# Routing logits of a fused attention and mixture-of-experts kernel: the gate's weight held in four column groups, and eight subtractions on GpSimd

## The chip, the cores and the metric

The kernel runs on one core of a Trainium2 chip. The metric is the device time of one execution in microseconds (us). The kernel before has a median of 2101.33 us over three runs (2100.89 to 2102.82).

## The reference, cut to what matters

Attention with 4 sink keys and a window of 128 (4 batches, 8 heads, 768 positions, 64 wide) gives x of 3072 tokens by 512. From x come the routing logits, which eight rounds of row and column scaling turn into the weights P of 8 experts; the output is the sum of P times each expert's result. The change touches the line that forms the logits, and the preparation of one expert's weights.

```python
attn_out = _attn_ref(q, k, v, n_sink, window)
x = attn_out.transpose(0, 2, 1, 3).reshape(B * S, H * D)      # 3072 x 512
logits = x @ w_gate                                           # 3072 x 8
P = np.exp(logits - logits.max())
for _ in range(8):
    P /= P.sum(1, keepdims=True) + 1e-09
    P /= P.sum(0, keepdims=True) + 1e-09
    P *= N / E
for e in range(E):
    out += P[:, e:e + 1] * (np.maximum(x @ w1[e], 0.0) @ w2[e])
```

## The kernel before, in words

The program has an attention part (up to about 262 us) and an expert part behind it. The attention part goes through 48 units: 24 blocks of 128 queries (4 batches of 6), each in two halves of four heads. Units run in a software pipeline. In `steady_round(n)` (units from 6 on) TensorE computes the scores of unit n+1 (`scores`, line 508, into the PSUM tiles st0 to st3, one per head), transposes the probabilities of unit n (`transpose_halves`, line 565), multiplies those of unit n-1 with V and then with the sinks' values (`values`, line 618), transposes the sinks' probabilities (`transpose_sinks`, line 583, into st0) and at the end takes two pieces of expert 0's first matmuls (`run_fill(2)`: lines 717 and 733), which are there to fill the round. VectorE adds the mask (`soften`, line 516), ScalarE takes the exponential (line 519), VectorE the reciprocal (lines 525 and 526), GpSimd scales (`divide`, line 528) and gathers the sinks (lines 577 and 578). Units 0 to 5 run in `early_round`, which has the same steps in a slightly different order, and after unit 48 a tail of fill pieces goes on together with the scaling of P.

On each engine the order is that in which the program issues the instructions (in the early rounds only TensorE's; a scheduler orders the others there), and an engine works strictly in its order: an instruction that waits holds up all that stand behind it. Small lists (`late`, `mid`, `coming`, `act_end`, `pool_end`) hold an instruction back until a set place of the round.

When both halves of a block are done, `put_x` stores the transposed x of its 128 tokens (the tile xr, 128 rows by 4 chunks `kc` by 128 tokens) and hands it to `run_gates` through `later` and `gates`. `run_gates(2)` stands at the head of a round and takes two such tiles, a **pair**; with 24 blocks there are 12 pairs, one in four rounds. It holds x stationary and streams the gate's weight, 8 columns wide, in two row halves (line 663), into the PSUM tiles t0 and t1, which `transpose_p` and `transpose_halves` also use. VectorE copies one half into Pt and adds the other (lines 667 and 668).

```python
for kc in range(KC):
    for j, (_, xr) in enumerate(pair):
        for lg, rows in zip(lgs, HALF):
            nc.tensor.matmul(lg[:, j, :], lhsT=xr[rows, kc, :], rhs=wg_raw[rows, kc, :], ...)
```

Expert 0's weights come in plain float32 and are split into a high part (a copy on ScalarE, line 693, through `act_end`) and a low part (a subtraction on VectorE, line 694, through `coming`). `in_turn` issues both for the piece that `PIECES` names for a unit: units 6 to 10, then 16, 18, 20, 22, 28, 30, 32 and 34. NB is 6.

Of the kernel before, what the change touches and what calls it, by code (L numbers as in the profile page):

```python
# [234 lines left out]
def tile_sink_attention_moe(ctx: ExitStack, tc: tile.TileContext, q, k, v, wg, w1, w2, out):  # L235
# [27 lines left out]
    def f32(ap):  # L263
        return ap.bitcast(F32)
# [44 lines left out]
                                             base=SINK - 1, channel_multiplier=-1).ins  # L309


    wg_raw = attc.tile([P, KC, E], F32, name="wg_raw")
    Xt = const.tile([P, NT + 1, E + 1], F32, name="Xt")

    const.tile([P, 8], F32, name="pad")
# [50 lines left out]
    def st_tile(shape, k=None):  # L366
        if k is None:
            k, turns[0] = turns[0] % 4, turns[0] + 1
        return ps_st.tile(shape, F32, name=f"st{k}")
# [227 lines left out]
    def values(n):  # L597

        b, i, hh = units[n]
        u = us[n]  # L600
        keys, ready, _ = due_keys(n)
        if not keys:
            return
        O = u["O"] = ps_o.tile([P, NP, 2, P], F32, name="O")
        u["side"] = {q_: j for j, q_ in enumerate(sorted(keys[0][1], key=lambda q_: spot(keys[0][0], keys[0][1][q_])))}
        ops = []
        for pr in range(NP):
            for m, qs in keys:
                R = spots(PTR[hh][:, 2 * pr:2 * pr + 2], [spot(m, s_) for s_ in qs.values()])
                sides = sorted(u["side"][q_] for q_ in qs)  # L610
                for h in range(2):
                    ops.append((O[h * D:(h + 1) * D, pr, sides[0]:sides[-1] + 1], raws[("vr", *units[m][:2])][:, hh * HH + 2 * pr + h, :], R[:, h]))
        for q_ in ready:
            if units[q_][1]:
                for pr in range(NP):
                    ops.append((O[:, pr, u["side"][q_]], seq[units[q_][0]][:, (hh * NP + pr) * P:(hh * NP + pr + 1) * P], us[q_]["PS"]))
        for j, (o_, x_, y_) in enumerate(ops):
            nc.tensor.matmul(o_, lhsT=x_, rhs=y_, start=(j < 2), stop=(j >= len(ops) - 2), skip_group_check=True)  # L618

    xrs = {}  # L620
# [20 lines left out]
    def put_x(n):  # L641
# [10 lines left out]
                pool_soon(lambda b_=b_, x_=x_: nc.gpsimd.tensor_sub(b_[:, 1, :, cols], x_, f32(b_[:, 0, :, cols])))  # L652
        later.append((tok // P, xr))

    def run_gates(least):

        while len(gates) >= least and gates:
            pair = [gates.pop(0) for _ in range(min(2, len(gates)))]
            lgs = [pst.tile([P, len(pair), E], F32, name=f"t{r}") for r in range(2)]
            for kc in range(KC):  # L660
                for j, (_, xr) in enumerate(pair):
                    for lg, rows in zip(lgs, HALF):
                        nc.tensor.matmul(lg[:, j, :], lhsT=xr[rows, kc, :], rhs=wg_raw[rows, kc, :],  # L663
                                         start=(kc == 0 and j == 0), stop=(kc == KC - 1), skip_group_check=True)
            t = pair[0][0]
            assert [t_ for t_, _ in pair] == list(range(t, t + len(pair)))
            nc.vector.tensor_copy(Pt[:, t:t + len(pair), :], lgs[0])
            nc.vector.tensor_add(Pt[:, t:t + len(pair), :], lgs[1], Pt[:, t:t + len(pair), :])

    WP, RP = {}, {}  # L670

# [17 lines left out]
        d = t[:, :, (j % 2) * KH:(j % 2 + 1) * KH] if j < 2 else t[:, :, j % 2]  # L689
        return d, RP[1, u][:, (j % 2) * KH:(j % 2 + 1) * KH] if j < 2 else RP[2, u][:, j % 2]  # L690

    def in_turn(d, src):
        act_end.append(lambda: nc.scalar.copy(d[:, 0], src))
        coming.append(lambda: nc.vector.tensor_sub(d[:, 1], src, f32(d[:, 0])))

    def split_first(j):

# [82 lines left out]
    def run_fill(k_):  # L780
        for _ in range(k_):
            next(fill, None)
# [52 lines left out]
    def early_round(n):  # L835

        if units[n + 2][2] == 0:
            with (tc.high_priority() if n == -2 else nullcontext()):
                for j in (0, 1) if n == -2 else (n // 2 + 2,) if n < 4 else ():
                    load_rows(("kr", "qr"), j)  # L840
                if n < 2:
                    load_rows(("vr",), n // 2 + 1)
                elif n == 4:
                    load_rows(("vr",), n // 2)
            if units[n + 2][1] == 0:
                load_sinks(units[n + 2][0])
        if n == 2:
            load_rows1(0)
        if n == 3:
            for j in (4, 5):  # L850
                load_rows(("kr", "qr"), j)
            load_rows1(1)
        ahead = nullcontext()
        if n in (3, 4):
            high, low_part = split_first(n - 3)
            ahead = tc.issue_after(high)
        squares_due(n)
        run_gates(2)
        if n == -2:
            nc.sync.dma_start(wg_raw, wg.rearrange("(k p) e -> p k e", p=P))  # L860
            spread_sinks(0)
            split_sinks(0)
            split_sinks_low(0)
        if n == 0:
            spin(1, 4)
            scores(1, 0)
            soften(1, (0, 1))
            spin(1, 4)
            scores(1, 1)
            spin(1, 4)  # L870
            transpose_qk(2)
            with tc.issue_after(us[0]["divided"]), tc.issue_after(us[2]["high"]):
                soften(1, (2, 3))
            divide(1, range(HH))
        elif on(n + 1):
            if n > 0:
                transpose_qk(n + 2)
            for pr in range(NP):
                scores(n + 1, pr)
                soften(n + 1, range(2 * pr, 2 * pr + 2))  # L880
            with ahead:
                divide(n + 1, range(HH))
            if 0 < n < 3:
                spare[0] = pst.tile([P, DM], F32, name="t1")
                spin(6 - n, 5)
        if on(n - 1):
            values(n - 1)
        for j in (0, 1) if n == -2 else ():
            transpose_qk(j)
        if on(n):  # L890
            transpose_p(n, 0)
            if units[n][1]:
                gather_sinks(n)
        if on(n):
            transpose_p(n, 1)
        if on(n - 1):
            store_x(n - 1)
        if on(n) and units[n][1]:
            transpose_sinks(n)
        if n >= START:  # L900
            run_fill(2)
        if n in (3, 4):
            behind_it, low = low_part(us[n + 1]["divided"])
            with behind_it:
                low()
        if n == STEADY - 1:
            split_second()
# [4 lines left out]
    def steady_round(n):  # L912
# [6 lines left out]
        if n in ROWS:  # L919
            ROWS[n][0](ROWS[n][1])  # L920
        squares_due(n)
        run_gates(2)
        if on(n + 1):
            for pr in range(NP):
                scores(n + 1, pr)
# [14 lines left out]
        flush(mid)  # L940
        if on(n - 1):
            values(n - 1)
        if on(n + 1):
            for pr in range(NP):
                divide(n + 1, range(2 * pr, 2 * pr + 2))
            if units[n + 1][1]:
                gather_sinks(n + 1)
# [9 lines left out]
        if on(n - 1):  # L957
            store_x(n - 1)
        if n < L:
            run_fill(2)  # L960
        if n in PIECES:
            in_turn(*plain_tiles(*PIECES[n]))
        if n == L - 8:
            first_pieces.extend(pieces1(0))
        if n == L - 2:
# [24 lines left out]
    with tc.manual_schedule():  # L990
# [8 lines left out]
            steady_round(n)  # L999
        gates += later  # L1000
        run_gates(1)
        for todo in (late, mid, coming):
            flush(todo)
        run_fill(1)
# [778 lines left out]
```

## Time and profile before

| | |
|---|---|
| median of three runs | 2101.33 us |
| the profiled execution's own time | 2101.58 us |
| its span | 2099.9 us |
| TensorE busy, share of the span | 2080.8 us, 99% |
| VectorE, ScalarE, GpSimd busy | 1481.1, 830.5, 700.0 us |
| mean granted TensorE clock | 0.996 |

In the rows, PE is TensorE's matmuls, PEld its weight loads, DVE VectorE, ACT ScalarE, POOL GpSimd; L663 is line 663 of the kernel. A shape is partitions by elements. "[1.46 <-DVE PT L554]" is the time that the engine stood idle ahead of the row and what ended it. A float32 matmul shows as two records, a transpose as one. In a merged row of the timeline the second number runs from the first start to the last modelled end, and matmuls overlap at their ends, so the distance to the next row's start is the time that a group really takes. PEclk is the granted clock as a share of 2.4 GHz, so 0.50 is 1.2 GHz.

### The profile page before, as it was taken

The numbers are of one execution on the slowest core, as the hardware profiler recorded it, in microseconds if no ns is written. First come the engines' busy times: TensorE is split into PE (matmuls) and PEld (weight loads), VectorE is DVE, ScalarE is ACT, GpSimd is POOL, SyncE is SP. The second block draws the span as 40 slices with busy tenths as digits, with TensorE's granted clock in tenths as the row PEclk, the third lists the DMA queues.
The fourth block names the chain that finished last, engine by engine and source line by source line (L and its number), as shares of the span: only waits on it lengthen the run. The fifth ranks groups of instructions, "written<-read, shape, count | busy, mean of one in ns | idle before, by whom it ended". The sixth has DMA issues, their size and how long they took to land.

```text
span 2099.9 us, 31828 instructions
## 1 busy us (share of the span) xinstructions
PE 2080.8 (99%) x10597; PEld 1708.3 (81%) x10597; DVE 1481.1 (71%) x2732; ACT 830.5 (40%) x1775; POOL 700.0 (33%) x856
## 2 busy tenths in 40 slices
PE   9999999999999999999999999999999999999998
PEld 6777788888888888888888888888888888888887
DVE  6777777777777776856766666766766666666666
ACT  6766635444444444432332233232432332233222
POOL 6655612323233231332223222323322232223223
PEclk9999999999999999999999999999999999999999
DMA  8656348989999897676666666668766666666662
GB/s 165 141 101 130 82 141 294 307 288 308 304 294 318 281 312 243 234 252 208 203 204 196 203 203 190 203 205 312 247 204 199 201 206 194 198 208 198 197 197 84
DMA packets 437275, 454.37 MB, mean 216 GB/s; under 512 B 139057, under 2 KB 305137, under 8 KB 436209
## 3 DMA queue, kind: packets, MB, share of 16 engines
q1 hardware_dynamic: 435128, 451.06, 69.7%
q8 instruction: 87, 1.43, 0.3%
q10 hardware_dynamic: 1976, 1.20, 0.2%
q14 instruction: 84, 0.68, 0.1%
HBM read 314.69 MB, written 137.46 MB: 215 GB/s over the span
## 4 chain that ended last, share of the span: by engine, by line
PE 92%; DVE 3%; ACT 3%; issue 1%; DMA 0%; SPq 0%; POOL 0%; ACTq 0%; DVEq 0%; POOLq 0%
PE c L1035 42%; PE o L1607 21%; PE held L1607 8%; PE held L1283 7%; PE o L1283 7%; ACT sc L519 2%; PE O L618 1%; PE t L663 1%; PE st L508 1%; PE f L733 1%; DVE sc L516 1%; PE f L717 1%; DVE PT L567 1%; PE st L717 1%; PE t L565 0%
## 5 line engine op out<-in xcount | busy, mean ns | idle before, releaser
L1061 ACT CAST hf<-w 128x512 fp32r<-128x512 f32 x448 | 265.3, 621 | 563.0 <-POOL w L1572 299.7
L1607 PE MATMUL o<-hf,W2q 128*128 128x512 f32 x1920 | 472.0, 390 | 0.0
L1607 PEld LDWEIGHTS o<-hf,W2q 128*128 128x128 f32 x1920 | 360.1, 188 | 75.4 <-DVE acc L1621 0.9
L1035 PE MATMUL c<-T,W1q 128*128 128x512 f32 x1530 | 388.9, 390 | 0.2 <-DVE w L1553 0.2
L1062 DVE TENSOR_TENSOR hf<-w,hf 128x512 fp32r<-128x512 f32 x448 | 329.4, 764 | 75.7 <-ACT hf L1061 68.2
L1035 PEld LDWEIGHTS c<-T,W1q 128*128 128x128 f32 x1530 | 286.9, 188 | 60.6 <-DVE w L1553 0.9
L1621 DVE TENSOR_TENSOR acc<-o,acc 128x512 f32<-128x512 f32 x298 | 204.8, 688 | 169.9 <-PE o L1607 169.7
L1035 PE MATMUL c<-B,W1q 128*128 128x512 f32 x1134 | 278.3, 390 | 0.0
L1035 PEld LDWEIGHTS c<-B,W1q 128*128 128x128 f32 x1134 | 212.6, 188 | 43.9
L1572 POOL TENSOR_TENSOR w<-w 128x512 f32<-128x512 f32 x64 | 82.7, 1292 | 492.0 <-DVE w L1554 481.1
L1553 DVE TENSOR_TENSOR w<-c,M 128x512 f32<-128x512 f32 x192 | 132.4, 689 | 137.7 <-PE c L1035 133.3
L1549 ACT COPY M<-c 128x512 f32<-128x512 f32 x192 | 112.8, 588 | 248.0 <-PE c L1035 247.9
L1607 PE MATMUL held<-hf,W2q 128*128 128x512 f32 x768 | 194.8, 390 | 0.0
L1035 PE MATMUL c<-T,W1f 128*128 128x512 f32 x672 | 170.9, 390 | 0.0
L1607 PEld LDWEIGHTS held<-hf,W2q 128*128 128x128 f32 x768 | 144.0, 188 | 29.8
L1589 POOL TENSOR_TENSOR w<-w 128x512 f32<-128x512 f32 x64 | 106.2, 1660 | 176.2 <-DVE hf L1062 176.2
L1283 PE MATMUL held<-W2f,h 128*128 128x512 f32 x648 | 164.6, 389 | 0.0
L1283 PE MATMUL o<-W2f,h 128*128 128x512 f32 x648 | 164.4, 389 | 0.0
L1035 PEld LDWEIGHTS c<-T,W1f 128*128 128x128 f32 x672 | 125.9, 188 | 26.3 <-issue 0.2
L1576 POOL TENSOR_TENSOR w<-w 128x512 f32<-128x512 f32 x64 | 83.7, 1308 | 176.3 <-DVE w L1554 172.1
L1283 PEld LDWEIGHTS o<-W2f,h 128*128 128x128 f32 x648 | 121.7, 188 | 25.2
L1283 PEld LDWEIGHTS held<-W2f,h 128*128 128x128 f32 x648 | 121.6, 188 | 25.2
(235 smaller groups left out, 2698.2 us busy)
## 6 DMA issues: line engine op xcount, KB each, us to landing
W2q<-w2s SPq DMA_DIRECT2D x448, 256.0 KB, 3.1
W1q<-w1s SPq DMA_DIRECT2D x444, 256.0 KB, 2.8
w1s<-W1f SPq DMA_DIRECT2D x56, 896.0 KB, 7.3
w2s<-WT SPq DMA_DIRECT2D x138, 256.0 KB, 3.4
r<-in_moe_w_dram SPq DMA_DIRECT2D x63, 512.0 KB, 4.1
w2s<-W2f SPq DMA_DIRECT2D x54, 256.0 KB, 5.4
PB<-psd SPq DMA_DIRECT2D x16, 512.0 KB, 4.7
xfs<-WT SPq DMA_DIRECT2D x56, 128.0 KB, 3.0
```

What stands on the lines that cost most here:

```text
L519: nc.scalar.activation(sc[:, h, :], sc[:, h, :], AF.Exp, bias=st[:, 0, h:h + 1], scale=-1.0, accum_out=st[:, 1, h:h + 1])
L1035: nc.tensor.matmul(ps, lhsT=w1(a, k), rhs=x[:, b, k, :], start=(start and j == 0), stop=(stop and j == len(TERMS) - 1), skip_group_check=n ...
L1061: nc.scalar.copy(dst[:, 0], src)
L1062: at(1, lambda: nc.vector.tensor_sub(dst[:, 1], src, f32(dst[:, 0])))
L1283: nc.tensor.matmul(o, lhsT=h[c, th][:, a, off:off + P], rhs=W2F[n, c][:, w, :], start=(begin and c == 0 and j == 0), stop=(end and c == 1 ...
L1549: nc.scalar.copy(t, T["c2"])
L1553: nc.vector.tensor_add(w, T["c1"], T[m])
L1572: nc.gpsimd.tensor_sub(S3, T["A11"], T["A21"])
L1576: nc.gpsimd.tensor_add(T["A21"], T["A21"], T["A22"])
L1589: at(k, lambda: nc.gpsimd.tensor_sub(T["A11"], w, T["A11"]))
L1607: nc.tensor.matmul(o, lhsT=W2Q[part, n, m][:, a, k * P:(k + 1) * P], rhs=F[part, n, H_OF[m]][:, w, :], start=(j == 0 and (begin or not hol ...
L1621: nc.vector.tensor_add(sums[m, k], o, sums[m, k])
```

## The change

The gate's weight `wg_raw` becomes 128 x 4 x 32, zero but for 8 of each 32 columns (a memset on GpSimd at the start, ahead of the weight's DMA). For a pair, `run_gates` now holds the weight of chunk kc stationary in column group kc (32 columns, output rows 32 kc to 32 kc + 31) and streams the 128 tokens of xr: 8 matmuls into st2. ScalarE copies the 128 x 256 result to `part`; later in the round two full transposes bring the tokens back onto the rows (into st3), and VectorE's `reduce_sum` adds the four groups up into Pt. The call moves from the head of the round to the middle of `values`, ahead of the sinks' matmuls, and the transposes back stand between the two fill pieces at the round's end (after the last pair: directly behind the gate). And from unit 13 on (8 of the 13 pieces) the low part is subtracted on GpSimd, through `pool_end`.

```diff
-    wg_raw = attc.tile([P, KC, E], F32, name="wg_raw")
+    GC = P // KC
+    wg_raw = attc.tile([P, KC, GC], F32, name="wg_raw")
+    nc.gpsimd.memset(wg_raw, 0.0)
...
         for j, (o_, x_, y_) in enumerate(ops):
+            if j == HH * len(keys):
+                run_gates(2)
             nc.tensor.matmul(o_, lhsT=x_, rhs=y_, start=(j < 2), stop=(j >= len(ops) - 2), skip_group_check=True)
...
     def run_gates(least):
...
-            lgs = [pst.tile([P, len(pair), E], F32, name=f"t{r}") for r in range(2)]
-            for kc in range(KC):
-                for j, (_, xr) in enumerate(pair):
-                    for lg, rows in zip(lgs, HALF):
-                        nc.tensor.matmul(lg[:, j, :], lhsT=xr[rows, kc, :], rhs=wg_raw[rows, kc, :],
-                                         start=(kc == 0 and j == 0), stop=(kc == KC - 1), skip_group_check=True)
...
-            nc.vector.tensor_copy(Pt[:, t:t + len(pair), :], lgs[0])
-            nc.vector.tensor_add(Pt[:, t:t + len(pair), :], lgs[1], Pt[:, t:t + len(pair), :])
+            lg = st_tile([P, k_, P], 2)
+            for j, (_, xr) in enumerate(pair):
+                for kc in range(KC):
+                    nc.tensor.matmul(lg[kc * GC:(kc + 1) * GC, j, :], lhsT=wg_raw[:, kc, :], rhs=xr[:, kc, :],
+                                     start=True, stop=True, skip_group_check=True)
+            part = att1.tile([P, 2, P], F32, name="part")[:, 0:k_]
+            nc.scalar.copy(part, lg)
+
+            def back(t=t, k_=k_, part=part):
+                ps = st_tile([P, k_, P], 3)
+                for j in range(k_):
+                    nc.tensor.transpose(ps[:, j, :], part[:, j, :], ident)
+                nc.vector.reduce_sum(Pt[:, t:t + k_, :], ps.rearrange("p t (g e) -> p t e g", e=GC)[:, :, 0:E, :], axis=AX.X)
+
+            turned_back.append(back)
...
-    def in_turn(d, src):
+    def in_turn(d, src, eng=nc.vector):
         act_end.append(lambda: nc.scalar.copy(d[:, 0], src))
-        coming.append(lambda: nc.vector.tensor_sub(d[:, 1], src, f32(d[:, 0])))
+        (coming if eng is nc.vector else pool_end).append(lambda: eng.tensor_sub(d[:, 1], src, f32(d[:, 0])))
...
     def steady_round(n):
...
-        run_gates(2)
...
         if on(n - 1):
             values(n - 1)
+        run_gates(2)
...
         if n < L:
-            run_fill(2)
+            run_fill(1)
+        flush(turned_back)
+        if n < L:
+            run_fill(1)
         if n in PIECES:
-            in_turn(*plain_tiles(*PIECES[n]))
+            in_turn(*plain_tiles(*PIECES[n]), nc.gpsimd if n > 2 * NB else nc.vector)
...
         run_gates(1)
+        flush(turned_back)
```

How the instructions stand at three places. TensorE in the round of the seventh pair, before (the line of dots leaves out the repetitions of a group):

```order
L663 MATMUL t_2882<-wg_raw,xr 128x8
L663 MATMUL t_2883<-wg_raw,xr 128x8
...
L508 MATMUL st_2904<-KQ_178 128x260
...
L565 MATMUL t_2912<-ident,sc 128x64
L565 MATMUL t_2913<-ident,sc 128x64
...
L618 MATMUL O<-PT_186,vr 64x256 x4
L618 MATMUL O<-PS,VS 128x128 x2
L583 MATMUL st_2961<-ident,SS_176 96x128
L733 MATMUL f<-W1f,h_1740 128x512 x6
```

and now, from the same round's values on (`part` is ScalarE's copy of the gate's result):

```order
L622 MATMUL O<-PT_187,vr 64x256 x4
L670 MATMUL st_2897<-xr,wg_raw 32x128 x8
L622 MATMUL O<-PS,VS 128x128 x2
L585 MATMUL st_2923<-ident,SS_177 96x128
L746 MATMUL f<-W1f,h_1726 128x512 x3
L678 MATMUL st_2934<-ident,part 128x128 x2
L746 MATMUL f<-W1f,h_1726 128x512 x3
L510 MATMUL st_2951<-KQ_183 128x260
```

Sixteen matmuls at the head of the round have become eight in its middle, and two transposes split the last fill piece from the one ahead of it.

ScalarE at the last pair, behind the last unit, before:

```order
L635 COPY xr<-O 128x256
L645 DMA xscr<-xr 128x4x128 x2
L693 CAST W1f<-r_3895 128x512 x2
L722 ACTIVATE h_4308<-st_4366 128x256
L1061 CAST T_4425<-x_4395 128x2x256 x2
```

and now:

```order
L639 COPY xr<-O 128x256
L649 DMA xscr<-xr 128x4x128 x2
L706 CAST W1f<-r_3851 128x512 x2
L673 COPY part<-st_4290 128x256
L735 ACTIVATE h_4254<-st_4307 128x256
```

The copy of the last gate's result stands behind two DMA issues and two casts; on TensorE the two transposes that read it stand directly behind that gate.

GpSimd around unit 28 (W is expert 0's first weight, r its raw float32 rows), before:

```order
L578 TENSOR_TENSOR SS_174<-sc,SS_174 128x16
L528 TENSOR_SCALAR sc<-sc,st 128x260 x4
L577 TENSOR_SCALAR SS_176<-sc 128x16 x2
L578 TENSOR_TENSOR SS_176<-sc,SS_176 128x16
L417 TENSOR_TENSOR vm<-vs,bd 96x512
```

and now:

```order
L530 TENSOR_SCALAR sc<-sc,st 128x260 x4
L579 TENSOR_SCALAR SS_177<-sc 128x16 x2
L580 TENSOR_TENSOR SS_177<-sc,SS_177 128x16
L707 TENSOR_TENSOR W_2670<-r_1239,W_2670 128x512
L530 TENSOR_SCALAR sc<-sc,st 128x260 x4
```

A subtraction of 128x512 now stands between the gathering of the sinks and the next unit's scaling.

## Rows read from the trace of the kernel before

**Rows 1.** Windows of 40 to 262 us: us, then busy time (instructions) per engine, clock, DMA share.

```profile
40.00:262.00 222.00, 215.36 (x2214) 167.86 (x2211) 166.23 (x678) 147.84 (x518) 132.90 (x310) 0.98 0.54 112
```

**Rows 2.** Timeline, seventh pair's round: start us, us, engine, line, operation.

```profile
166.37 1.96 PE L663 MATMUL t<-wg_raw,xr 64*128 64x8 f32 x32
168.18 1.13 PE L508 MATMUL st<-KQ 64*128 64x260 f32 x8
171.69 0.19 ACT L519 ACTIVATION_READ_ACCUMULATOR sc<-sc,st 128x1 f32 x1
172.78 1.15 PE L508 MATMUL st<-KQ 64*128 64x260 f32 x8
```

**Rows 3.** Line 663: who waited for it (us, times).

```profile
  DVE Xt L667: 20.1, 12
```

**Rows 4.** Groups by line and form, 0 to 262 us: busy us, mean ns.

```profile
L618 PE MATMUL O<-PT,vr 128*64 128x256 f32 x288 | 41.8, 406 | 0.0
L618 PE MATMUL O<-PT,vr 128*64 128x128 f32 x128 | 11.7, 290 | 0.0
L635 ACT COPY xr<-O 128x256 f32<-128x256 f32 x48 | 16.8, 367 | 5.1 <-DVE xr L631 4.5 <-POOL sc L528 0.6
```

**Rows 5.** Timeline, TensorE: eight records of 128 columns; eight transposes.

```profile
41.25 0.66 PE L618 MATMUL O<-PT,vr 128*64 128x128 f32 x8
41.84 0.31 PE L583 MATMUL st<-ident,SS 128*96 128x128 f32 x1
...
27.55 1.06 PE L550 MATMUL t<-ident,sc 128*128 128x128 f32 x8
28.45 0.27 PE L583 MATMUL st<-ident,SS 128*96 128x128 f32 x1
```

**Rows 6.** Timeline, weight loads behind a change of column groups.

```profile
175.36 0.30 PEld L618 LDWEIGHTS O<-PS,VS 96*128 96x128 f32 x2 [0.38 <-issue]
```

**Rows 7.** Timeline, first pair: ScalarE frees st0; the next scores.

```profile
29.57 0.26 ACT L585 CAST PS<-st 96x128 fp32r<-96x128 f32 x1
33.42 2.10 PE L508 MATMUL st<-KQ 64*128 64x260 f32 x8
```

**Rows 8.** Windows of 2 us behind three gates; PEclk is the third number from the end.

```profile
130.00:132.00 2.00, 2.00 (x10) 0.89 (x6) 1.53 (x10) 1.86 (x9) 0.76 (x3) 0.50 0.64 122
190.00:192.00 2.00, 2.00 (x22) 1.50 (x23) 1.87 (x11) 0.93 (x5) 0.00 (x0) 0.50 0.62 100
262.00:264.00 2.00, 2.00 (x11) 2.00 (x10) 1.48 (x3) 0.16 (x2) 0.00 (x0) 0.50 1.05 336
```

**Rows 9.** Timeline, scores of 128 columns: the round behind a gate, then one without.

```profile
127.94 0.70 PE L508 MATMUL st<-KQ 64*128 64x128 f32 x8
133.64 0.71 PE L508 MATMUL st<-KQ 64*128 64x128 f32 x8
...
65.99 0.71 PE L508 MATMUL st<-KQ 64*128 64x128 f32 x8
70.28 0.72 PE L508 MATMUL st<-KQ 64*128 64x128 f32 x8
```

**Rows 10.** Timeline, last pair.

```profile
259.42 1.95 PE L663 MATMUL t<-wg_raw,xr 64*128 64x8 f32 x32
260.99 1.14 ACT L693 CAST W1f<-r 128x512 fp32r<-128x512 f32 x2 [0.64 <-ACT xr L635]
261.30 2.63 PE L717 MATMUL st<-B,W 128*128 128x256 f32 x12
```

**Rows 11.** Timeline: a subtraction on VectorE; the gates of the sixth and eighth pair.

```profile
172.81 0.73 DVE L694 TENSOR_TENSOR W<-r,W 128x512 fp32r<-128x512 f32 x1
...
146.26 1.95 PE L663 MATMUL t<-wg_raw,xr 64*128 64x8 f32 x32
187.46 1.96 PE L663 MATMUL t<-wg_raw,xr 64*128 64x8 f32 x32
```

**Rows 12.** Groups by line and form, 0 to 262 us: GpSimd's subtraction of 128x512.

```profile
L1221 POOL TENSOR_TENSOR x<-x,x 128x512 f32<-128x512 f32 x6 | 7.9, 1356 | 0.1
```

More of the change, by code (lines that the diff above doesn't have):

```diff
@@ L653, in put_x @@
         later.append((tok // P, xr))
+    turned_back = []
     def run_gates(least):
@@ L658, in run_gates @@
             pair = [gates.pop(0) for _ in range(min(2, len(gates)))]
-            lgs = [pst.tile([P, len(pair), E], F32, name=f"t{r}") for r in range(2)]
-            for kc in range(KC):
-                for j, (_, xr) in enumerate(pair):
-                    for lg, rows in zip(lgs, HALF):
-                        nc.tensor.matmul(lg[:, j, :], lhsT=xr[rows, kc, :], rhs=wg_raw[rows, kc, :],
-                                         start=(kc == 0 and j == 0), stop=(kc == KC - 1), skip_group_check=True)
-            t = pair[0][0]
-            assert [t_ for t_, _ in pair] == list(range(t, t + len(pair)))
-            nc.vector.tensor_copy(Pt[:, t:t + len(pair), :], lgs[0])
-            nc.vector.tensor_add(Pt[:, t:t + len(pair), :], lgs[1], Pt[:, t:t + len(pair), :])
+            t, k_ = pair[0][0], len(pair)
+            assert [t_ for t_, _ in pair] == list(range(t, t + k_))
+            lg = st_tile([P, k_, P], 2)
[11 more added lines that the diff above has]
+            turned_back.append(back)
     WP, RP = {}, {}
@@ L857, in early_round @@
         squares_due(n)
-        run_gates(2)
         if n == -2:
-            nc.sync.dma_start(wg_raw, wg.rearrange("(k p) e -> p k e", p=P))
+            nc.sync.dma_start(wg_raw[:, :, 0:E], wg.rearrange("(k p) e -> p k e", p=P))
             spread_sinks(0)
@@ L900, in early_round @@
         if n >= START:
-            run_fill(2)
+            run_fill(1)
+        flush(turned_back)
+        if n >= START:
+            run_fill(1)
         if n in (3, 4):
@@ L921, in steady_round @@
         squares_due(n)
-        run_gates(2)
         if on(n + 1):
@@ L942, in steady_round @@
             values(n - 1)
+        run_gates(2)
         if on(n + 1):
@@ L959, in steady_round @@
         if n < L:
-            run_fill(2)
+            run_fill(1)
+        flush(turned_back)
+        if n < L:
+            run_fill(1)
         if n in PIECES:
-            in_turn(*plain_tiles(*PIECES[n]))
+            in_turn(*plain_tiles(*PIECES[n]), nc.gpsimd if n > 2 * NB else nc.vector)
         if n == L - 8:
@@ L1001, in tile_sink_attention_moe @@
         run_gates(1)
+        flush(turned_back)
         for todo in (late, mid, coming):
```

## The prediction

> **What bounds the kernel now.** I read the windows first. From 40 to 262 us, the attention part's steady stretch, TensorE is busy for 215.4 of 222 us at a clock of 0.98, VectorE for 166, ScalarE for 148, GpSimd for 133 and the DMA engines for 54% [rows 1]. So TensorE's own work is the bound, 6.6 us are its idle time, and a microsecond that leaves its order there is worth nearly a microsecond, as long as the chain scores, mask, exponential, scaling keeps up. Behind 262 us nothing is changed and TensorE is as full, so what is won at 262 us should reach the end.
>
> Then the timeline of one round. The seventh pair's gate starts at 166.37 and the scores behind it at 168.18: 1.81 us of TensorE for 32 records that stream 8 columns each [rows 2]. The round's next scores come at 172.78. VectorE, which reads the gate at the round's head, stands still meanwhile: 20.1 us over the 12 pairs [rows 3].
>
> Last the clock. In 2 us windows I see it at 0.50, the lower of its two levels (1.2 GHz), behind four of the twelve gates, the first, fifth, eighth and last; rows 8 show three of them. What TensorE did just before each time is the gate. The round behind the fifth gate takes 133.64 - 127.94 = 5.70 us; one of the same make (128 columns of keys, a fill of line 733, no gate ahead) takes 70.28 - 65.99 = 4.29 us [rows 9]. One drop costs 1.4 us.
>
> **The change, part by part.** The sum is made against the profiled execution's own time, 2101.58 us, which lies 0.25 us above the median.
>
> *A pair's price, new.* No row shows four column groups. Two groups are shown: records of line 618 last 406 ns at 256 columns and 290 ns at 128 [rows 4], so 128 columns of a float32 record stream for 116 ns. Eight such records on two groups, four on each, take 41.84 - 41.25 = 0.59 us [rows 5]; one after another they would stream for 8 x 0.116 = 0.93 us, so the two groups do run side by side. The new gate has 16 records on four groups, again four on each. I take 0.59 us, since a group's own series is no longer. Upper bound: nothing side by side, 16 x 0.116 = 1.86 us. Two at a time would be 8/4 x 0.59 = 1.18 us.
>
> The two transposes back: eight of 128x128 take 28.45 - 27.55 = 0.90 us [rows 5], so 0.23 us for two. They split two fill pieces and need no other cover.
>
> The gate now stands between matmuls of another column width, one more change of width per pair. Behind such a change the weight load of the sinks' matmuls stands idle for 0.38 us [rows 6], mostly while earlier matmuls still run; as a cost on TensorE I bound it by 0 and 0.38 and take 0.1, nearer to 0 because the matmuls themselves show no gap there.
>
> The Trainium skill speaks against this change here: TensorEngine Tiling (Array Packing), Key Properties, has a change of tiling mode drain the engine. The trace agrees in so far as the load waits, 0.38 us; by the rule taken in full, 11 pairs would lose another 0.28 us each, 3 us in all.
>
> So a pair goes from 1.81 to 0.59 + 0.23 + 0.1 = 0.92 us and saves 0.89. Pairs 2 to 11 are ten such: **-8.9 us** (-10 to +7).
>
> *The first pair.* It stands in an early round. TensorE is done with unit 3's sinks at 28.45 + 0.27 = 28.72 and starts the next scores only at 33.42, because the gate first waits for VectorE to free t0 and t1. Without a gate there the scores wait for four transposes and for ScalarE's copy that frees st0, which ends at 29.57 + 0.26 = 29.83 [rows 5, 7]. That is 3.5 us, less 0.92 for the new gate in the same round. The clock drop behind this gate adds an estimated half of the 1.4 us, 0.7, as these early rounds wait on other engines more than the later ones do: **-3.3 us** (-1 to -4).
>
> *The clock.* If what set the clock down is the gate's stretch of very narrow matmuls, the drops behind the fifth and eighth gate go with it: 2 x 1.4 = **-2.8 us** (0 to -2.8).
>
> *The last pair.* Before, TensorE goes on with the fill 261.30 - 259.42 = 1.88 us after the gate's start. Now the transposes stand directly behind the gate and need ScalarE's copy, which stands behind casts that end at 260.99 + 1.14 = 262.13 [rows 10]. The copy of 128x256 takes 0.37 us (as line 635 does) [rows 4], the transposes 0.23: the fill goes on at about 262.8, **+1.5 us** (0.5 to 3). The clock drop at 262 [rows 8] may stay, since TensorE stands idle for some 2 us instead; I leave it as it is.
>
> *The eight subtractions.* On VectorE one takes 0.73 us and stands in front of the next round's masks [rows 11]. Gate to gate, the stretch from the sixth to the seventh pair, with one subtraction in a round that has room, takes 166.37 - 146.26 = 20.11 us; the next, with two, 187.46 - 166.37 = 21.09 [rows 2, 11]. So one that falls in a tight round costs TensorE about 0.98 us, and one in a round with room nothing. I take two of the eight as tight, **-2.0 us** (0 to -2.5). On GpSimd the same shape takes 1.36 us [rows 12], between a unit's gathering of the sinks and the next unit's scaling; GpSimd is busy only 60% of the stretch [rows 1], and if that cover is gone TensorE's transposes wait for the scaling, up to 8 x 1.36 = 11 us.
>
> *Nothing, because covered:* ScalarE's copies (11 x 0.37 us, ScalarE 67% busy) and VectorE's reductions, which replace two small instructions and a wait of 1.7 us per pair [rows 3]. The memset at the start delays only the load of the gate's weight, which the first pair is the first to want. The DMA count is the same.
>
> Sum: -3.3 - 8.9 - 2.8 + 1.5 - 2.0 = -15.5. 2101.58 - 15.5 = 2086.1, and less the 0.25 that the profiled execution lies above the median: **2086 us**.
>
> **The rivals.**
>
> *Column groups share less than I think.* For it: nothing shows four at once. Against it: two groups do run side by side [rows 5]. At two at a time each of the 12 gates costs 0.59 more: 2086 + 7 = 2093 us. With no overlap at all it is 1.27 more, 15 us: about 2101 us, no change, and the change would not do what its layout is for.
>
> By TensorE: Matmul & The Clock Gate, Part 3, What overlaps and what doesn't, the Trainium skill has a weight load overlap running matmuls only where the row group differs; column groups share all rows, so by it this rival gains. The trace does not bear the strict form out: loads of two column groups in the same rows take no more room than 0.59 - 4 x 0.116 = 0.13 us [rows 4, 5].
>
> *The clock drops stay,* because it is the attention part's many short matmuls and not the gate. For it: eight gates are followed by no drop. Against it: all four drops lie directly behind a gate. 2086 + 2.8 = 2089 us.
>
> *The gate becomes a wait, and the kernel slower.* TensorE works in order, and the gate is now in the middle of the round: it needs st2, which VectorE frees with its third mask, and the transposes back need ScalarE's copy, which stands behind the next unit's four exponentials, with one fill piece between. In the old round the last exponential was read out at 171.69 + 0.19 = 171.88, which is 3.7 us after the scores' start at 168.18 [rows 2]; with the copy 4.1. TensorE reaches the transposes back about 4.5 us after the scores' start (4.6 for the old round, less half a fill of 0.8, plus the gate's 0.7). The margin is 0.4 us, and VectorE no longer waits for the gate, which adds to it. If the copy came late by w, 11 pairs lose 11 w; the gain is gone at w = 15.5 / 11 = 1.4 us, and at w = 2 it is 2086 + 22 = 2108 us. Against it speaks that margin.
>
> **How the numbers follow.** My forecast has 0.70, two column groups at a time 0.12, clock drops that stay 0.08, no overlap 0.06, the wait 0.04. A measurement can tell some 0.2% from no change, 4.2 us: below 2097.1 counts as faster, above 2105.5 as slower. The first three cases are faster, 0.90; no overlap is the same, 0.06; the wait is slower, 0.04. The range's lower end takes the best price of each part: ten pairs at -10, the first at -4, the subtractions at -2.5, the clock at -2.8 with the drop at 262 gone too (-1.4), the last pair at +0.5, and some of the 6.6 us of idle time, 1.5: about -21.5, 2080 us. The upper end takes two groups at a time and 2 us more of waits: 2095 us. That leaves out the last two cases and the ends of the others, not more than 2 in 10.
>
> **What would show it.** The gate's records should fill about 0.6 us from their start to the next kind's, the two transposes 0.23. A round with its gate should last about 5.5 us, not 172.78 - 166.37 = 6.4 [rows 2]. No window at 0.50 should lie in the middle of the attention part. The last unit's fill should end about 14 us earlier than before, and the stretch behind it should last as long as before, within 1 us or so. GpSimd's scaling should not be what TensorE's transposes of line 565 wait for. I am wrong if the gate takes over 1.1 us, if TensorE waits for ScalarE's copy in every pair, or if the stretch behind 262 us grows by what the attention part wins.

## The result and the profile after

The changed kernel takes 2081.7 us (median of 4 runs, 2080.42 to 2084.09); the kernel before took 2101.63 in the same comparison. The ratio is 0.9906, with a 95% interval of 0.9889 to 0.9923: about 20 us faster. The forecast was 2086 us, and the time lies in its range of 2080 to 2095. The profiled execution took 2081.61 us with a span of 2079.9, against 2101.58 and 2099.9, so the traces differ by 20.0 us.

TensorE's order in the seventh pair's round, and ScalarE and VectorE beside it (timeline of the changed kernel: start us, us, engine, line, operation); it answers to [rows 2]:

```profile
152.47 1.15 PE L510 MATMUL st<-KQ 64*128 64x260 f32 x8
155.05 0.64 PE L670 MATMUL st<-xr,wg_raw 128*32 128x128 f32 x16
155.63 0.44 PE L622 MATMUL O<-PS,VS 96*128 96x128 f32 x2
155.94 0.95 PE L746 MATMUL f<-W1f,h 128*128 128x512 f32 x3
156.72 0.38 PE L678 MATMUL st<-ident,part 128*128 128x128 f32 x2
156.86 0.95 PE L746 MATMUL f<-W1f,h 128*128 128x512 f32 x3
157.74 0.49 PE L510 MATMUL st<-KQ 64*128 64x260 f32 x2
...
155.78 0.35 ACT L673 COPY part<-st 128x256 f32<-128x256 f32 x1
...
157.43 0.22 DVE L679 TENSOR_REDUCE Xt<-st 128x16 f32<-128x64 f32 x1
```

The gate (line 670) takes 155.63 - 155.05 = 0.58 us from its start to the sinks' matmuls, where the old one took 1.81. ScalarE's copy ends at 156.13, and TensorE reaches the transposes at 156.72: a margin of 0.59 us. The round lasts 157.74 - 152.47 = 5.27 us.

The windows, the attention part up to 240 us, the stretch that answers to [rows 1], and one behind the last gate (us, busy per engine, clock third from the end):

```profile
20.00:240.00 220.00, 212.32 (x2193) 162.21 (x2189) 174.53 (x701) 163.17 (x571) 151.85 (x345) 1.00 0.62 129
40.00:243.00 203.00, 196.26 (x2019) 149.55 (x2017) 161.56 (x648) 147.41 (x516) 135.66 (x307) 0.99 0.61 126
242.00:244.00 2.00, 2.00 (x10) 1.90 (x10) 0.22 (x1) 0.30 (x2) 0.00 (x0) 0.50 0.07 21
```

TensorE is as full as in [rows 1], but the work fits into about 20 us less. From 20 to 240 us the clock is 1.00 on the mean: the drops behind the first, fifth and eighth gate [rows 8] are gone; the one behind the last is not.

What TensorE's matmuls wait for between 20 and 243 us, the three largest of ten rows (view of waits: us in total, times, longest):

```profile
PE st L678 <- ACT part L673: 2.0, 2, 1.6
PE f L730 <- DVE h L736: 1.7, 4, 0.5
PE t L567 <- DVE PT L569: 1.0, 1, 1.0
```

None of the ten names GpSimd. The 1.6 us for ScalarE's copy is the last pair:

```profile
236.99 0.41 PE L670 MATMUL st<-xr,wg_raw 128*32 128x128 f32 x4
237.58 0.82 PE L670 MATMUL st<-xr,wg_raw 128*32 128x128 f32 x12 [0.17 <-DVE xr L635]
240.02 0.44 PE L678 MATMUL st<-ident,part 128*128 128x128 f32 x2 [1.63 <-ACT part L673]
...
239.61 0.36 ACT L673 COPY part<-st 128x256 f32<-128x256 f32 x1
```

To see where the 20 us come from I compare the starts of the scores, round by round. The third to the tenth pair lie between these starts, before and after (timelines; each row is the head of a round):

```profile
77.89 1.15 PE L508 MATMUL st<-KQ 64*128 64x260 f32 x8
161.40 1.15 PE L508 MATMUL st<-KQ 64*128 64x260 f32 x8
182.12 1.15 PE L508 MATMUL st<-KQ 64*128 64x260 f32 x8
243.68 1.15 PE L508 MATMUL st<-KQ 64*128 64x260 f32 x8
```

```profile
72.87 1.15 PE L510 MATMUL st<-KQ 64*128 64x260 f32 x8
147.96 1.15 PE L510 MATMUL st<-KQ 64*128 64x260 f32 x8
166.73 1.15 PE L510 MATMUL st<-KQ 64*128 64x260 f32 x8
221.53 1.15 PE L510 MATMUL st<-KQ 64*128 64x260 f32 x8
```

These eight pairs took 165.79 us and take 148.66, 17.1 less; the seventh alone, which met no clock drop in either, 182.12 - 161.40 = 20.72 and 166.73 - 147.96 = 18.77. Worked out the same way, the two rounds of the first pair gain 4.2 us, the second pair 0.7, the eleventh 0.3. The last pair loses 1.9: from its gate to the matmul of line 35 behind it took 265.75 - 259.42 = 6.33 us and takes 245.22 - 236.99 = 8.23, both with a clock drop in it. Behind that the traces differ by half a microsecond.

### The profile page after: what moved, and what is told of

It reads as the page before. It is cut to its first block, busy times and chain, and to the rows that moved or that the text cites. A ratio compares the mean times of both kernels' runs of the same rounds, so it can differ in the third digit from the quotient of the medians.

```text
span 2079.9 us, 31459 instructions
## 1 busy us (share of the span) xinstructions
PE 2061.2 (99%) x10429; PEld 1689.7 (81%) x10429; DVE 1477.3 (71%) x2712; ACT 833.9 (40%) x1787; POOL 706.3 (34%) x865
## 4 chain that ended last, share of the span: by engine, by line
PE 95%; ACT 2%; DVE 2%; issue 0%; DMA 0%; POOL 0%; ACTq 0%; DVEq 0%; POOLq 0%
PE c L1055 42%; PE o L1627 21%; PE held L1627 8%; PE held L1303 7%; PE o L1303 7%; PE O L622 2%; ACT sc L521 2%; PE st L510 1%; PE f L746 1%; PE f L730 1%; PE st L730 1%; DVE sc L518 1%; PE t L567 1%; DMA vr<-in_v_dram 0%; PE t L746 0%
```

## The experiments

Theory: the column form makes each gate cheaper by the predicted 0.9 us, its place keeps TensorE from waiting in the first pair, the subtractions give 2 us, and the clock drops go with the narrow matmuls. The rivals: the place or VectorE's freedom is worth more than the form; the subtractions are worth nothing, or all; the clock has another cause. The medians of before, beside which they ran, were 2102.58 us (e1, e2, e5, e7), 2102.68 (e3, e4, e6) and 2102.41 (the others). This table sets the runs side by side; its stretches are worked out from the starts of the scores as above.

| run | gate | place | subtractions | median us | ratio (95%) | pairs 3 to 10, us | pairs 5 + 6 | pair 7 |
|---|---|---|---|---|---|---|---|---|
| before | x stationary | head | VectorE | 2101.6 | 1 | 165.79 | 40.56 | 20.72 |
| e2 | x stationary | head | GpSimd | 2098.7 | 0.998 (0.9971 to 0.9989) | 161.76 | 38.82 | 19.89 |
| e3 | x stationary, VectorE free | head | VectorE | 2099.4 | 0.9986 (0.9977 to 0.9995) | 161.55 | 39.02 | 20.41 |
| e4 | x stationary, 32 columns | head | VectorE | 2101.3 | 0.9992 (0.9983 to 1.0001) | 169.37 | 40.25 | 20.76 |
| e5 | x stationary | middle | GpSimd | 2093.7 | 0.9962 (0.995 to 0.9974) | 157.38 | 37.70 | 19.82 |
| e6 | column groups | head | GpSimd | 2087.0 | 0.9923 (0.9909 to 0.9936) | 152.49 | 36.55 | 19.07 |
| e1 | column groups | middle | VectorE | 2083.4 | 0.9906 (0.9891 to 0.9921) | 150.35 | 36.08 | 19.13 |
| after | column groups | middle | GpSimd | 2081.7 | 0.9906 (0.9889 to 0.9923) | 148.66 | 35.66 | 18.77 |

**e1, the gate without the subtractions.** The changed kernel with all low parts on VectorE:

```diff
-            in_turn(*plain_tiles(*PIECES[n]), nc.gpsimd if n > 2 * NB else nc.vector)
+            in_turn(*plain_tiles(*PIECES[n]))
```

> The changed kernel with all thirteen low parts back on VectorE; the gate as changed. Theory (the subtractions cost TensorE time only in tight rounds, some 0.35 to 0.7 us each, five or six of the eight): 2 to 3.5 us above the changed kernel's 2081.7, so about 2084.5 us, with rounds of 4.8 us again where a subtraction stands in front of the masks. Rival (the gate alone freed VectorE so far that the subtractions no longer cost anything): 2081 to 2082 us, and those rounds at 4.5 us.

Measured: 2083.4 us, between the two expectations. The medians and intervals do not tell it from the changed kernel (both ratios are 0.9906), but the traces do: pairs 3 to 10 take 150.35 us, 1.7 more. Nearly all of it sits in four rounds ahead of a gate that hold a subtraction, 0.37 to 0.43 us each; the pieces in other rounds cost next to nothing. So beside the new gate the subtractions are worth 1.7 us; that its sign is right the trace alone shows.

**e2, the subtractions without the gate.** The kernel before with `in_turn` as in the change:

```diff
-        coming.append(lambda: nc.vector.tensor_sub(d[:, 1], src, f32(d[:, 0])))
+        (coming if eng is nc.vector else pool_end).append(lambda: eng.tensor_sub(d[:, 1], src, f32(d[:, 0])))
```

> The kernel before with only the eight low parts on GpSimd. Theory: 2 to 3 us below before, about 2099 us; the round behind the seventh gate's goes from 4.84 to 4.5 us. Rival (GpSimd comes late with the scaling, TensorE's transposes wait for it): no gain or a loss, 2101 us or more, and waits of line 565 for the scaling.

Measured: 2098.7 us, 3.9 below before, where 2 to 3 were expected. But not all of that is VectorE's room: the clock moved too. Its windows of 2 us:

```profile
84.00:86.00 2.00, 1.90 (x9) 1.90 (x10) 1.43 (x7) 1.42 (x6) 1.48 (x4) 0.50 1.23 276
130.00:132.00 2.00, 2.00 (x25) 1.33 (x20) 1.97 (x12) 1.23 (x7) 0.00 (x0) 1.00 0.62 102
190.00:192.00 2.00, 2.00 (x11) 1.42 (x9) 1.53 (x8) 2.00 (x9) 1.02 (x3) 1.00 0.66 131
```

The old gate stands where it stood, with its 8 columns, and yet the drops at 130 and 190 us are gone, and one at 84 us is new. In the first pair the clock is down for longer than in before: its two rounds take 15.88 us, not 14.29. In the seventh pair, where before had no drop, the two subtractions gave 20.72 - 19.89 = 0.83 us; beside the new gate, in e1, they cost 19.13 - 18.77 = 0.36.

**e5, the old gate in the new place.** The changed kernel with the x-stationary gate, whose sums VectorE takes out where the reduction stood:

```diff
+            lgs = [st_tile([P, k_, E], 2 + r) for r in range(2)]
...
+                        nc.tensor.matmul(lg[:, j, :], lhsT=xr[rows, kc, :], rhs=wg_raw[rows, kc, 0:E],
...
+            def back(t=t, k_=k_, lgs=lgs):
+                nc.vector.tensor_copy(Pt[:, t:t + k_, :], lgs[0])
+                nc.vector.tensor_add(Pt[:, t:t + k_, :], lgs[1], Pt[:, t:t + k_, :])
```

> The changed kernel with the old form of the gate (x stationary, 8 columns streaming, 32 records) at the new place in the middle of the round, in st2 and st3, its copy and addition on VectorE where the reduction stands now. Theory (the column groups are worth 1.8 - 0.87 us a pair, and the narrow matmuls set the clock down): rounds with a gate at about 6.0 us instead of 5.0 to 5.3, a drop of the clock behind a few gates again, in sum 8 to 14 us above the changed kernel, 2090 to 2096 us. Rival (the place is what gains, by freeing VectorE at the round's head): within 4 us of the changed kernel, 2082 to 2086 us.

Measured: 2093.7 us, as the theory had it. In its seventh pair (timeline) the gate is the old one, 162.70 - 160.82 = 1.88 us:

```profile
160.82 1.96 PE L671 MATMUL st<-wg_raw,xr 64*128 64x8 f32 x32
162.70 0.44 PE L622 MATMUL O<-PS,VS 96*128 96x128 f32 x2
```

Pairs 3 to 10 take 157.38 us, 8.72 more than with the column form: 1.09 us per pair, and the clock is no part of it: over those pairs it is 1.00 in this profile too (windows):

```profile
74.50:231.88 157.38, 154.38 (x1618) 120.18 (x1617) 125.90 (x521) 111.43 (x396) 102.17 (x244) 1.00 0.58 119
```
The median says 12 us for the form, but this kernel's runs lie between 2090.65 us, with a mean granted clock of 0.999, and 2099.99, with 0.994. The profiled one is the fastest; its span of 2088.9 us is 9.0 above the changed kernel's. So the form's price is taken from the traces. The drops that the theory expected are not in this one.

**e6, the new gate in the old place.** The changed kernel with `run_gates(2)` moved back to the head of the round; the transposes back stay at its end.

```diff
-            if j == HH * len(keys):
-                run_gates(2)
...
+        run_gates(2)
```

> The changed kernel with the new gate in the old place, at the head of a round, before its scores; copy by ScalarE, transposes back and reduction follow in the same round, subtractions on GpSimd. Theory (the form saves and the place adds little, since ScalarE's copy has time behind the gate and VectorE is not held): 2081 to 2085 us. Rival (the place is what keeps VectorE and ScalarE clear of the round's masks): rounds with a gate 0.4 to 1 us longer than in the changed kernel, 2086 to 2093 us.

Measured: 2087.0 us, the rival's range at its lower edge. Against the changed kernel pairs 3 to 10 take 3.83 us more, 0.48 per pair; against e2, the old gate in the same place, 161.76 - 152.49 = 9.3 less, or 8.1 without the 1.2 us by which the drop at 84 makes e2's third pair longer than that of before: 1.01 per pair. That comparison holds more than the form, since in e6 VectorE no longer waits for the gate at the round's head. Its view of waits between 60 and 236 us has a row that the changed kernel's lacks:

```profile
PE st L510 <- ACT part L671: 0.9, 3, 0.5
```

At the head of the round the scores wait for ScalarE to have taken the gate's sums out of the tile that they are to write. The row holds only 0.9 of the 3.83 us, but the seventh pair's whole loss sits in the same place: from the gate's start over the scores to the transposes TensorE takes 157.71 - 155.85 = 1.86 us, where the changed kernel takes 0.58 for the gate and 148.94 - 147.96 = 0.98 for scores without one. These 0.30 us are all that this pair loses. The other pairs are not taken apart here.

**e3, VectorE set free of the old gate.** The kernel before, where ScalarE copies the two halves and GpSimd adds them:

```diff
-            nc.vector.tensor_copy(Pt[:, t:t + len(pair), :], lgs[0])
-            nc.vector.tensor_add(Pt[:, t:t + len(pair), :], lgs[1], Pt[:, t:t + len(pair), :])
+            both = att1.tile([P, 2, 2, E], F32, name="both")[:, :, 0:len(pair)]
+            nc.scalar.copy(both[:, 0], lgs[0])
+            nc.scalar.copy(both[:, 1], lgs[1])
+            nc.gpsimd.tensor_add(Pt[:, t:t + len(pair), :], both[:, 0], both[:, 1])
```

> The kernel before, where VectorE no longer takes the gate's sums out of PSUM at the head of a round: ScalarE copies both halves and GpSimd adds them up; gate, order and subtractions stay as they are. Theory (part of what a pair cost before was VectorE standing behind the gate, which makes the following round 4.60 us long in place of 4.23): the rounds behind a gate fall to 4.2 to 4.3 us in about nine pairs, 3 to 4 us in all, 2097.5 to 2099.5 us. Rival (the longer round is TensorE's own, and VectorE's wait is covered, as the prediction had it): the rounds stay at 4.60 and the time is 2101 to 2103 us, or above if ScalarE's two copies come in the way.

Measured: 2099.4 us. The sixth pair's round behind the gate, before and in e3 (timelines, heads of rounds):

```profile
148.07 1.13 PE L508 MATMUL st<-KQ 64*128 64x260 f32 x8
152.67 1.15 PE L508 MATMUL st<-KQ 64*128 64x260 f32 x8
```

```profile
148.24 1.13 PE L508 MATMUL st<-KQ 64*128 64x260 f32 x8
152.52 1.15 PE L508 MATMUL st<-KQ 64*128 64x260 f32 x8
```

4.60 us become 4.28, with TensorE's own order unchanged. The way leads through VectorE's queue: behind the gate's sums stand the masks, and behind these the low part of h (line 723, in e3 725), which the fill at the round's end reads (line 733, in e3 735). VectorE and TensorE's weight loads in this round, before and in e3 (timelines):

```profile
150.61 0.42 DVE L723 SCALAR_TENSOR_TENSOR h<-f,h 128x256 fp32r<-128x256 f32 x1
151.08 0.53 PEld L733 LDWEIGHTS f<-W1f,h 128*128 128x128 f32 x3 [0.33 <-DVE h L723]
```

```profile
150.94 0.53 PEld L735 LDWEIGHTS f<-W1f,h 128*128 128x128 f32 x3
```

The weight loads of this line wait for h in three rounds of before, 0.33 us each, and in none of e3 or of the changed kernel. In the pairs that carry two subtractions the gain is split: 0.16 to 0.18 us in this round, 0.15 in the next. So a wait of VectorE (with the two small instructions behind it), which the prediction had costed at nothing, cost TensorE about 0.3 us per pair in the pairs that met no drop (4, 7 and 10). The two middle drops are gone here too, with the old gate's matmuls untouched: pairs 5 and 6 take 39.02 us instead of 40.56, 1.54 less, for VectorE's wait and one drop together. What each of them is worth shows only beside e4.

**e4, the old gate four times as wide.** The kernel before with the gate's weight padded with zeros to 32 columns:

```diff
+    GC = P // KC
-            lgs = [pst.tile([P, len(pair), E], F32, name=f"t{r}") for r in range(2)]
+            lgs = [pst.tile([P, len(pair), GC], F32, name=f"t{r}") for r in range(2)]
```

> The kernel before with the gate's moving weight padded with zeros from 8 to 32 columns: the same 32 records per pair in the same place, each four times as wide. Theory as the prediction had it (the 8-column records set TensorE's clock down behind the fifth and the eighth gate): both windows of 0.50 go, the gate stays at 1.8 to 1.9 us, and the time is 2097 to 2100 us. Rival (the two drops hang on where the rounds fall in time, not on the width; moving the subtractions alone has already taken both away and put one elsewhere): windows of 0.50 remain in the attention, there or at another gate, and the time is 2101 to 2104 us.

Measured: 2101.3 us, the interval of its ratio reaching 1.0001: no change that can be told. Windows of 2 us:

```profile
82.00:84.00 2.00, 2.00 (x11) 2.00 (x12) 1.37 (x5) 1.18 (x5) 1.72 (x4) 0.55 1.29 245
90.00:92.00 2.00, 2.00 (x22) 1.41 (x21) 1.52 (x10) 2.00 (x9) 0.39 (x1) 0.50 0.78 136
130.00:132.00 2.00, 2.00 (x39) 2.00 (x37) 0.23 (x2) 0.53 (x2) 0.72 (x4) 1.00 0.65 161
```

The middle drops go, as they did in e2 and e3, and a longer one comes at 82 to 92 us: the rival. The timeline shows the third gate and the fifth:

```profile
84.46 3.63 PE L665 MATMUL t<-wg_raw,xr 64*128 64x32 f32 x32
...
129.66 1.98 PE L665 MATMUL t<-wg_raw,xr 64*128 64x32 f32 x32
131.46 0.69 PE L510 MATMUL st<-KQ 64*128 64x128 f32 x8
```

The clock is down before 84 us, and that gate starts at 84.46, so it did not set this drop off.

But for the gate's width, e4 is from its fourth pair on the kernel before without the two middle drops: the pairs that meet none in either run, 4, 7 and 10, take 21.17, 20.76 and 20.91 us here and 21.13, 20.72 and 20.94 in before. So it prices a drop. Pairs 5 and 6 lie between the two scores here, and the row between them is in the round of the sixth pair's gate (timeline):

```profile
124.31 1.15 PE L510 MATMUL st<-KQ 64*128 64x260 f32 x8
145.07 1.03 PE L567 MATMUL t<-ident,sc 64*128 64x64 f32 x16 [0.32 <-DVE PT L569]
164.56 1.15 PE L510 MATMUL st<-KQ 64*128 64x260 f32 x8
```

They take 40.25 us, only 0.31 less than in before; pairs 8 and 9 take 0.36 less. The round with the drop becomes 1.3 us shorter (5.70 to 4.39), but in the next ones TensorE comes to wait for VectorE; in before, it seems, VectorE caught up while the clock was down. So a drop cost 0.3 to 0.4 us there, net. And VectorE's wait, with no drop on either side, was worth more than 0.3: pairs 4 to 10 take 143.35 us in e4 and 140.02 in e3, 0.48 per pair, of which the wider gate is 0.04 at most.

**b1 and a1, the two kernels again.** No edit.

> The kernel before once more, to see whether TensorE's clock falls at the same places in a second profile of the same program. Theory as the prediction had it (the fifth and the eighth gate set the clock down): windows of 0.50 behind the gates near 126 and 187 us again, and the round behind each 5.7 us. Rival (where it falls differs from one execution to the next, and no one gate causes it): other windows, for instance near 84 us, where two other variants with the same waits fell; the rounds behind the fifth and the eighth gate are then 4.4 us. The time is that of before, 2101 to 2104 us, either way.

> The changed kernel once more. Theory (it has no clock drop in the attention because the 8-column records are gone): 1.00 in every window up to 236 us, 2080 to 2084 us. Rival (the drops hang on where an execution's waits fall): a window of 0.50 somewhere in the attention, or none behind the last pair, which has one in the first profile; the time moves by no more than 1.5 us per drop.

Measured: 2102.4 us (ratio 1.0, 0.9989 to 1.001) and 2080.1 us (0.9892, 0.9873 to 0.9912). In b1 the middle drops are back at the same gates, within a few tenths of a microsecond:

```profile
130.00:132.00 2.00, 2.00 (x9) 0.86 (x10) 1.53 (x13) 1.89 (x9) 0.43 (x2) 0.50 0.56 97
192.00:194.00 2.00, 2.00 (x10) 1.13 (x7) 1.53 (x8) 1.58 (x7) 1.04 (x3) 0.50 0.70 140
```

So the rival, that they would fall elsewhere, is not borne out. That every execution has the same drops is not shown: b1's eight timed runs have mean granted clocks of 0.996 to 0.998. In a1 there is none in the attention, nor behind the last pair:

```profile
242.00:244.00 2.00, 2.00 (x14) 1.64 (x13) 1.21 (x4) 1.25 (x3) 0.00 (x0) 1.00 0.14 42
```

so that one does differ between executions of one program. From the last gate to line 35 a1 takes 243.93 - 237.23 = 6.70 us, not 8.23: that drop is worth 1.5 us. Before has one too in its 6.33 us; e2 and e3, with the old gate and no drop there, take 4.81 (e2: 261.68 - 256.87).

**e7 and e8, the copy on VectorE.** The changed kernel with `part` copied by VectorE, in the last pair alone (e7) or in all (e8):

```diff
-            nc.scalar.copy(part, lg)
+            (nc.scalar.copy if least == 2 else nc.vector.tensor_copy)(part, lg)
```

```diff
-            nc.scalar.copy(part, lg)
+            nc.vector.tensor_copy(part, lg)
```

> The changed kernel with the last pair's copy on VectorE instead of ScalarE. Theory (the last pair costs 1.9 us more than before because the copy stands behind two casts of ScalarE): the transposes back start some 1.1 us earlier, TensorE stands idle for 0.5 us instead of 1.6, and the drop of the clock behind it may go too: 1 to 2.5 us below the changed kernel, about 2080 us. Rival (VectorE is then late with the scaling of P): no gain, 2081.7 us.

> The changed kernel with the copy of the new gate's sums on VectorE in all twelve pairs, in place of ScalarE. The prediction costed ScalarE's copies at nothing. Theory (true but for the last pair, where TensorE waits 1.6 us for it; on VectorE the copy delays masks and sums instead): the last pair's gain of 1 to 2 us is there, each other pair loses 0 to 0.3 us, 2079.5 to 2083 us. Rival (ScalarE is late in other pairs too, and VectorE has room now that it waits for no gate): below the variant with only the last copy moved (2079.8 us), 2076 to 2079 us.

Measured: 2079.8 us (ratio 0.9894, 0.9878 to 0.9909) and 2078.9 us (0.9886, 0.987 to 0.9903). In e7 the last pair's wait is 0.5 us, not 1.6 (view of waits, from 230 us):

```profile
PE st L678 <- DVE part L673: 0.5, 1, 0.5
```

and from the last gate to line 35 it takes 243.14 - 237.53 = 5.61 us, 1.1 less than a1. In e8 pairs 3 to 10 take 148.69 us, as in the changed kernel (148.66): which of the two engines copies costs nothing there. So e8's median lies in the rival's range, but the rival's reason, a ScalarE that is late in other pairs too, is not seen. Both are the fastest versions tried, but their intervals overlap with the changed kernel's; the 1.1 us rests on the traces.

## Why the prediction was right, and where it was wrong

The direction, the mechanism of the gate and the range held; the gain was 20 us and not 15.5. Term by term:

*A pair's price.* Right, and a little low. The gate took 0.58 us where 0.59 was taken from two groups, so four groups do share the array. The form alone saved 1.09 us per pair in the middle (after against e5), and 1.01 at the head (e6 against e2), where VectorE's wait goes with it; the prediction had 1.81 - 0.59 - 0.23 = 0.99, less 0.1 for the change of width. That 0.1 is not seen. By TensorEngine Tiling (Array Packing), Key Properties, of the Trainium skill a change of tiling mode drains the engine, which the prediction put at 3 us over 11 pairs; the traces show no such loss. In TensorE: Matmul & The Clock Gate, Part 3, What overlaps and what doesn't, the Trainium skill speaks of weight loads, which overlap running matmuls only where the row group differs. Read as a bar to column groups running side by side, it would have meant the rival without overlap, an estimated 16 x 0.116 = 1.86 us per gate; the measured 0.58 excludes that here, with the sixteen weight loads, all on the same rows, done in 0.38 of it (PEld, 155.05 us).

*"Nothing, because covered."* This is the step that failed. It set VectorE's wait of 1.7 us per pair [rows 3] at zero because VectorE is not the bound. But VectorE waits at the head of a round, and behind that wait stand the masks and the low part of h, for which the fill's weight loads then wait. Taking this wait away won 0.3 us per pair where before met no drop, and 0.48 over pairs 4 to 10 against e4. The whole move of the old gate to the middle was worth 0.40 us per pair (e2, without its drop, against e5). The move of the new one was worth 0.48 (e6 against after), but there another wait goes, the scores' for ScalarE's copy. In eight pairs that is 3.2 to 3.8 us that stand in no term of the sum.

*The subtractions.* Sized 2.0 us by two tight rounds. In pairs 4 to 10, with no drop on either side, they gave 143.35 - 138.73 = 4.6 us alone (e4 against e2): four pairs, 4, 5, 7 and 8, won 0.87 to 1.12 us each. Beside the new gate they gave 1.7. The price of them depends on what else holds VectorE: the pair with two of them gained 0.83 us beside the old gate, 0.36 beside the new one.

*The clock.* The two middle drops are gone, but not for the reason given. They also went with the old gate and its 8 columns in place (e2, e3), and with 32 columns a longer one came. One cost 0.3 to 0.4 us, not 1.4, since the rounds behind it give most of it back (e4). The prediction compared one round with one round. The term was 2.8 and measured 0.7; its cause stays open.

So for pairs 3 to 10: from before to e2 5.2 us (165.79 - 161.76, and the 1.2 of e2's own drop), of which two drops are 0.7 and the subtractions 4.5; from there to the changed kernel 160.56 - 148.66 = 11.9, of which 8.1 is form and 3.8 place by e6, or 8.7 and 3.2 by e5. Together 17.1. The shares hold for this order of steps; taken last, the subtractions give 1.7. The prediction had 7.1 + 2.8 + 2.0 = 11.9 for the same stretch. Its clock was 2.1 too large and its subtractions 2.5 too small: that these two nearly cancel is luck, and the missing place is most of what is left.

*The first pair.* 4.2 us instead of 3.3. In e4, whose first pair met no drop, it took 12.40 us where before took 14.29, but the round behind gave 0.4 back (5.34 against 4.90), so the drop there is likely worth nearer 1.5 than the 0.7 that was assumed. The gate's wait for t0 and t1 went with the tile and not with the place: in e6 the gate stands at the head, in st2, and the three rounds from there take 14.64 us, 14.65 in the changed kernel. The second pair gave 0.7, in the repeat 1.0. The eleventh gave 0.3: the values ahead of its gate now wait 0.9 us for VectorE's xr, a wait that before does not show.

*The last pair.* Lost 1.9 us, predicted 1.5; it is ScalarE's copy standing behind the casts, as said. Without a drop on either side the loss is the same, 6.70 - 4.81 = 1.9 (a1 against e2). On VectorE the copy gives 1.1 of it back (e7).

*The gate becomes a wait.* Did not come: the copy had a margin of 0.59 us where 0.4 was worked out. With the gate at the head (e6) TensorE's scores did wait for it.

*GpSimd.* No transpose came to wait for a scaling that had not waited before, as forecast: the weight loads of the transposes wait for GpSimd's scaling in five places, 2.3 us, before and now alike. Its subtractions (groups by line and form, changed kernel: busy us, mean ns) took 1.28 us where [rows 12] had 1.36:

```profile
L707 POOL TENSOR_TENSOR W<-r,W 128x512 fp32r<-128x512 f32 x4 | 5.1, 1279 | 0.2 <-ACT W L706 0.2
```

## What to carry to other kernels

An engine at 75% can still cost the bound engine time: ask not how busy it is but what stands in its queue behind the waiting instruction. Here 1.7 us of VectorE's waiting per pair, with the masks and the fill's h behind it, cost TensorE 0.3 to 0.5 us, and moving the gate away from the head of the round paid over a third of what making it cheaper did. Price a clock drop by a kernel in which it and nothing else is missing, over several rounds, since what waits meanwhile may catch up, and do not tie it to the instruction in front of it before a run has changed that instruction alone.

## What the runs showed of the hardware that was not expected

Four column groups, 128 rows each, ran sixteen float32 records of 128 columns in 0.58 us, 36 ns a record; two groups took as long, 0.59 us, for eight [rows 5].

The old gate's price did not hang on its columns: with 32 instead of 8, a record lasted 273 ns instead of 253 (medians), but the 32 of a pair still took 131.46 - 129.66 = 1.80 us (e4, timeline), as the 1.81 of [rows 2].

TensorE's granted clock fell to 0.50 behind the same two gates in both profiles of before, and behind neither in e2, e3, e4, e5 or the changed kernel, although e2 and e3 leave that gate and its place as they were. In e2 it fell near 84 us instead. TensorE's timeline there, in e2 and in before:

```profile
81.53 1.03 PE L565 MATMUL t<-ident,sc 64*128 64x64 f32 x16 [1.03 <-DVE PT L567]
...
84.10 2.93 PE L717 MATMUL f<-B,W 128*128 128x256 f32 x12 [0.46 <-DVE h L723]
```

```profile
80.04 1.03 PE L565 MATMUL t<-ident,sc 64*128 64x64 f32 x16 [1.00 <-DVE PT L567]
...
82.61 1.68 PE L717 MATMUL f<-B,W 128*128 128x256 f32 x12 [0.46 <-DVE h L723]
```

The same two waits stand ahead of the same twelve matmuls, which took 2.93 us in one and 1.68 in the other. So neither the narrow gate nor these waits decide it alone. What sets the clock down in this kernel was not found.
